# Two MLPs after linear attention in fp32 by three products: the first layer's blocks 7 and 8 as a pair by seven products of halves

## The chip, the core and the metric

The kernel runs on one core of a Trainium2 chip. The metric is the device time of one execution in microseconds, as the median of three runs. The engines are TensorE (PE in the rows, its weight loads PEld), VectorE (DVE), ScalarE (ACT), GpSimd (POOL) and SyncE (SP), which here only starts DMA transfers.

## What is computed

```python
kv = einsum('bhsd,bhse->bhde', k, v)           # 8 batches, 8 heads, 576 tokens, 64 wide
o  = einsum('bhsd,bhde->bhse', q, kv)
x  = o / sqrt(mean(o*o, -1) + 1e-6) * g_norm   # -> 4608 tokens x 512
h  = x @ w_in                                  # 512 x 2048
x1 = where(h >= 1, h, where(h <= -1, 0, (h + 1)**2 / 4)) @ w_out      # 2048 x 512
y  = maximum(x1 @ w_in2, 0)**2 @ w_out2
```

The weights come as 64-bit floats, which the kernel narrows to fp32 itself.

## The kernel before, in words

**Arithmetic.** A matrix of fp32 numbers is kept as a high part, rounded to TensorE's fp32r, and the rest, its low part. A product is three matmuls, high by high, high by low and low by high (`mm3`, L193 to 196; `mm_group`, L762 to 770 in the second layer). Making the two parts takes a cast on ScalarE and a subtraction on VectorE (`split`, `halve`).

**Blocks.** The 4608 tokens are nine blocks of 512: block b below 8 has the first 512 tokens of batch b, block 8 the last 64 tokens of every batch, which are gathered in DRAM (`xrd`). The first layer goes through the blocks in order, and each has 16 steps of 128 hidden features. A step issues `h_stage` (L576 to 597: 12 matmuls into one of two banks, then relu with a bias and a square on ScalarE, and a minimum and maximum on VectorE, giving u), `g_stage` (the two parts of u, named gs) and, two steps behind, `out_stage` (L606: 12 matmuls of gs and the step's output weights into four banks). Attention of batch b + 1 is made in block b, at fixed half-steps: `kv_stage`, `t_stage` (the transposed q), `o_stage` and `r_stage` (the norm). The results of a block go to DRAM (`x1d<-ev`), as does each batch's leftover (`xrd<-xrem`). In block 0 the first layer's weights are still being loaded, narrowed and split (`load_w`, `split_w`), beside attention 0 and 1.

**Second layer.** Blocks 0 to 7 go in four pairs. Pair n makes both of its blocks at once by seven products of halves (Strassen's scheme in Winograd's form, `PRODUCTS`, L73): tokens, inputs and hidden features are cut in two, sums of quarters are made of the inputs and of the weights, and 7 products stand where 8 would. `in_phase` (L783) makes the hidden features in four quarters of seven products by two feature steps; `out_phase` (L836) makes the seven output products one after the other. Each phase has 336 matmuls of 128x512. Block 8 follows as a plain block with streamed weights (`ws<-wcd`).

**Weights of the pairs.** The sums of the second layer's weights do not depend on the tokens. They are made in blocks 1 to 7 of the first layer by 16 jobs (`prep_load`, `prep_narrow`, `prep_sums`, `prep_split`, L264 to 316), one for each pair of weight tiles: load and narrow two tiles, four sums of 128x256, four splits, and stores to DRAM (`wsd<-s` for the products, `wcd<-s` whole for block 8), all started on SP's queue. The pairs then stream them, 512 KB at a time, through a ring of eight tiles (`ws<-wsd`). So that the jobs have room, the last six tiles of the first layer's output weights are stored as well (`wtd<-w`) and loaded again in each block (`wt<-wtd`).

**What sets the order.** The code is written in the order of a table of half-steps (`hook`), and a scheduler keeps this order on each engine but for priorities in the first block. All engines wait on semaphores and take their instructions in order. Tiles are handed round in pools and rings, so that a load waits until its tile is free. The transfers use eight semaphores in turn, over all queues, and a transfer is started only when the one that used its semaphore before has landed.

## Time and profile before

| | |
|---|---|
| median of three runs | 1597.66 us (1597.16 to 1598.02) |
| profiled execution, its own time | 1595.62 us |
| its span | 1593.8 us |
| TensorE busy, share of the span | 1577.4 us, 99% |
| VectorE, ScalarE, GpSimd busy | 949.1, 910.5, 111.0 us |
| mean DMA rate | 190 GB/s |

The span runs from the first to the last recorded instruction. Matmuls are pipelined and overlap in the records, so the pace of TensorE is read from the starts of groups of matmuls and not from the duration of one. In a timeline row the bracket at the end is idle time of the engine ahead of the row and what ended it.

### The profile page before, as it was taken

Reading aid. Unit: us, or ns where it says so; the run is one execution under the profiler, and the core shown is the slowest. Engines: PE = TensorE matmul, PEld = TensorE weight load, DVE = VectorE, ACT = ScalarE, POOL = GpSimd, SP = SyncE. Lnnn points to the kernel's source line nnn. Section 1 sums busy time; section 2 is a strip of 40 time slices with the busy share of each in tenths; the row PEclk is TensorE's granted clock in tenths of the full one; section 3 lists DMA queues with packets and bytes.
Section 4 is the critical chain, followed back from the end, with each engine's and each line's share of the span. In section 5 each row is a group of like instructions: output and inputs, shape, how many; then the busy total and the mean of one; then the engine's idle time right before and its main releaser. Section 6 shows DMA issues by size and latency. Waiting matters only on the chain.

```text
span 1593.8 us, 21182 instructions
## 1 busy us (share of the span) xinstructions
PE 1577.4 (99%) x7539; PEld 1292.1 (81%) x7541; DVE 949.1 (60%) x1574; ACT 910.5 (57%) x1661; POOL 111.0 (7%) x105
## 2 busy tenths in 40 slices
PE   9999999999999999999999999999999999999998
PEld 5678888888888888888888888888888888888886
DVE  6996656657666576643244348744974496457522
ACT  5986756667666676644344556456636663665321
POOL 0000000000000000000000121012101300330000
PEclk9999999999999999999999999999999999999999
DMA  9926567675776757522140557686768666865773
GB/s 285 280 83 174 195 170 228 179 239 174 228 215 186 235 177 230 182 73 90 53 145 29 170 194 242 194 219 222 237 195 243 218 216 198 243 219 186 201 239 102
DMA packets 306969, 302.36 MB, mean 190 GB/s; under 512 B 195504, under 2 KB 248752, under 8 KB 306864
## 3 DMA queue, kind: packets, MB, share of 16 engines
q1 hardware_dynamic: 304880, 300.22, 61.2%
q8 instruction: 60, 0.98, 0.2%
q10 hardware_dynamic: 1984, 0.79, 0.2%
q14 instruction: 45, 0.37, 0.1%
HBM read 231.74 MB, written 69.21 MB: 189 GB/s over the span
## 4 chain that ended last, share of the span: by engine, by line
PE 71%; issue 15%; DVE 9%; ACT 3%; POOL 1%; DMA 1%; DVEq 0%; SPq 0%; POOLq 0%; ACTq 0%
PE acc L196 26%; PE ph L196 26%; PE ph L770 10%; PE po L770 4%; DVE t L715 3%; DVE x L715 1%; PE po L196 1%; PE pkv L417 1%; POOL t L831 1%; DVE g L860 1%; PE pr L520 1%; DMA xr<-x1d 1%; DVE xr L738 1%; PE pwarm L1013 1%; ACT raw L226 1%
## 5 line engine op out<-in xcount | busy, mean ns | idle before, releaser
L196 PE MATMUL ph<-x,w 128*128 128x512 f32 x1728 | 418.9, 391 | 4.5 <-ACT w L175 2.0
L196 PEld LDWEIGHTS ph<-x,w 128*128 128x128 f32 x1728 | 321.7, 188 | 72.5 <-ACT w L175 2.9
L770 PE MATMUL po<-t,ws 128*128 128x512 f32 x1344 | 307.3, 391 | 1.7 <-DVE t L715 1.7
L770 PE MATMUL ph<-x,ws 128*128 128x512 f32 x1344 | 306.5, 390 | 0.7 <-DVE e L815 0.7
L770 PEld LDWEIGHTS po<-t,ws 128*128 128x128 f32 x1344 | 251.6, 188 | 56.7 <-DVE t L715 4.9
L770 PEld LDWEIGHTS ph<-x,ws 128*128 128x128 f32 x1344 | 252.2, 188 | 54.0 <-DVE e L815 1.9
L196 PE MATMUL acc<-gs,w 128*128 128x512 f32 x1152 | 281.2, 392 | 0.2 <-DVE u L594 0.2
L196 PEld LDWEIGHTS acc<-gs,w 128*128 128x128 f32 x1152 | 213.6, 188 | 43.7 <-DVE u L594 0.8
L592 ACT ACTIVATE u<-ph,halfb 128x512 f32<-128x512 f32 x144 | 99.3, 690 | 183.6 <-PE ph L196 183.2
L594 DVE SCALAR_TENSOR_TENSOR u<-u,ph 128x512 f32<-128x512 f32 x144 | 98.6, 684 | 167.7 <-ACT u L182 167.4
L715 DVE TENSOR_TENSOR t<-g,t 128x512 fp32r<-128x512 f32 x192 | 134.8, 708 | 74.2 <-ACT t L175 70.4
L175 ACT CAST t<-g 128x512 fp32r<-128x512 f32 x192 | 116.4, 620 | 71.8 <-DVE t L715 51.6
L188 DVE TENSOR_TENSOR gs<-u,gs 128x512 fp32r<-128x512 f32 x160 | 110.5, 690 | 62.2 <-ACT gs L175 61.3
L175 ACT CAST gs<-u 128x512 fp32r<-128x512 f32 x160 | 99.4, 621 | 74.4 <-DVE u L594 57.3
L196 PE MATMUL acc<-gs,wt 128*128 128x512 f32 x576 | 139.4, 391 | 0.0
L196 PEld LDWEIGHTS acc<-gs,wt 128*128 128x128 f32 x576 | 106.9, 188 | 21.5
L823 DVE TENSOR_TENSOR h<-ph,e 128x512 f32<-128x512 f32 x96 | 66.0, 691 | 55.9 <-PE ph L770 50.2
L824 ACT ACTIVATE h<-h 128x512 f32<-128x512 f32 x96 | 60.5, 630 | 60.0 <-DVE h L823 56.1
L182 ACT ACTIVATE u<-u 128x512 f32<-128x512 f32 x144 | 91.0, 632 | 2.0
L831 POOL TENSOR_TENSOR t<-g 128x512 f32<-128x512 f32 x32 | 43.1, 1346 | 633.7 <-ACT g L825 353.0
L825 ACT ACTIVATE g<-h 128x512 f32<-128x512 f32 x128 | 80.9, 632 | 3.6
L815 DVE TENSOR_TENSOR e<-ph,e 128x512 f32<-128x512 f32 x64 | 43.4, 688 | 44.3 <-PE ph L770 43.3
(108 smaller groups left out, 1427.3 us busy)
## 6 DMA issues: line engine op xcount, KB each, us to landing
ws<-wsd SPq DMA_DIRECT2D x224, 512.0 KB, 3.3
wsd<-s SPq DMA_DIRECT2D x112, 256.0 KB, 4.1
wt<-wtd SPq DMA_DIRECT2D x48, 512.0 KB, 4.5
raw<-in_moe_w_in_dram SPq DMA_DIRECT2D x32, 512.0 KB, 5.7
raw<-in_moe_w_out_dram SPq DMA_DIRECT2D x32, 512.0 KB, 5.5
wcd<-s SPq DMA_DIRECT2D x32, 512.0 KB, 3.2
ws<-wcd SPq DMA_DIRECT2D x32, 512.0 KB, 3.5
x1d<-ev SPq DMA_DIRECT2D x36, 256.0 KB, 3.1
```

The costliest lines, as they stand in the source:

```text
L175: return e.copy(dst, src)
L182: e.activation(dst, src, AF.Square)
L188: lo = engine(op + "_lo", phase).tensor_tensor(t[:, 1, :], src, t[:, 0, :].bitcast(F32), ALU.subtract)
L196: nc.tensor.matmul(dst, wt(a), xt(c), start=first and n == 0, stop=last and n == 2)
L592: nc.scalar.activation(u, ps, AF.Relu, bias=halfb, scale=0.5)
L594: nc.vector.scalar_tensor_tensor(u, u, 1.0, ps, op0=ALU.min, op1=ALU.max)
L715: engine2(op + "_lo").tensor_tensor(t[:, 1, :], src, t[:, 0, :].bitcast(F32), ALU.subtract)
L770: nc.tensor.matmul(ps, wt(a), xt(c), start=first and n == 0 and i == 0, stop=last and n == len(lhs) - 1 and i == 2, skip_group_check=True,)
L823: nc.vector.tensor_tensor(h, bank, add, ALU.add)
L824: nc.scalar.activation(h, h, AF.Relu)
L825: nc.scalar.activation(g, h, AF.Square)
L831: engine2("t_sum").tensor_tensor(t1[k], b, a, ALU.subtract)
```

## The change

The first layer's blocks 0 to 6 stay plain. Its blocks 7 and 8 are made as a pair, by the code that made the second layer's pairs, and the pairs run in this order: second layer 0 and 1, 2 and 3, first layer 7 and 8, second layer 4 and 5, 6 and 7. The second layer's block 8 is still plain.

- Attention 7, in block 6, writes its result to DRAM (`xpd`, from `xt`) and the pair loads its inputs from `xpd` and `xrd` as the others do from `x1d`.
- All streamed weights lie in one set of DRAM arrays, `wsd[layer, in or out, quarter]`, and tiles have the halves of features outside: `[128, half, high or low, 256]`. `wcd` and `wtd` are gone.
- The first layer's split weights are kept in DRAM as well (`keep_halves`, `keep_first`), and its sums are made by the same 16 jobs: `prep_join` adds the two parts of a tile again, `prep_sums` and two `prep_split` follow. All jobs are spread over 164 half-steps, from half-step 36, where they were spread over 104 steps.
- The tail of output weights that are loaded again in each block is nine tiles and not six; the jobs use five tiles of a ring and not three.
- The stores of sums, of kept weights and of the results of plain blocks are queued in a list (`owed`) and started half a step later on ScalarE's queue (`pay`).
- In the first layer's pair each of the four products of a feature step that end in the activation has relu with a bias and the square on ScalarE, and a minimum and maximum on VectorE. `put_out` stores its results without the transposes.

```diff
-    TAIL = 6
-    RING = 3
+    TAIL = 9
+    RING = 4
...
+    PLAIN = B - 1
+    PAIRS = [(2, 0), (2, 2), (1, PLAIN), (2, 4), (2, 6)]
...
+    def keep_halves(L, which, i, n, t):
+
+        made = MADE[which][2 * n : 2 * n + 2]
+        hs = slice(0, 2)
+        if L == 1 and None in made and not (which == 1 and i + n * NH >= NF - TAIL):
+            hs = slice(1, 2) if made[0] is None else slice(0, 1)
+        owed.append(
+            (wsd[L, which, i // 2][:, 2 * n + hs.start : 2 * n + hs.stop, i % 2], t[:, hs])
+        )
+
+    owed = []
+
+    def pay(n):
+
+        for dst, src in owed[:n]:
+            nc.scalar.dma_start(dst, src)
+        del owed[:n]
...
-            nc.sync.dma_start(wtd[f - (NF - TAIL)], t.rearrange("p a f -> p (a f)").bitcast(F32))
+            keep_halves(L, which, f % NH, f // NH, t.bitcast(F32))
...
+    def prep_join(L, which, i):
+
+        for n in range(2):
+            f = i + n * NH
+            t = prep.get((L, which, i, n))
+            if t is not None:
+                d, w = t[:, :, 0, :], t
+            else:
+                w = (wi[L, f] if which == 0 else wo[L, f]).bitcast(F32)
+                d = d_tile(f"j_{which}_{f}").rearrange("p (h f) -> p h f", h=2)
+            nc.vector.tensor_tensor(d, w[:, :, 0, :], w[:, :, 1, :], ALU.add)
+            prep[L, which, i, n] = d
...
+    def prep_split(L, which, i, n):
+        src = prep.pop((L, which, i, n))
+        t = prep_tile(f"s{L}_{which}_{i}_{n}", [P, 2, 2, H2], F32R)
+        split_halves(t, src, engine2("s_hi"), engine2("s_lo"))
+        keep_halves(L, which, i, n, t.bitcast(F32))
+
+    def keep_first(which, f):
+
+        t = wi[1, f] if which == 0 else wo[1, f]
+        keep_halves(1, which, f % NH, f // NH, t.bitcast(F32))
...
-        norm(t, y, o)
-        nc.gpsimd.tensor_copy(xrem[b][:, hp, :], t[:, TB:])
-        split(xs[1, b][hp], t[:, :TB], "x", b)
+        if b < LAST_B:
+            norm(t, y, o)
+            nc.gpsimd.tensor_copy(xrem[b][:, hp, :], t[:, TB:])
+            split(xs[1, b][hp], t[:, :TB], "x", b)
+            return
...
         if L == 1:
-            nc.sync.dma_start(x1d[b][:, c, :], t)
+            owed.append((x1d[b][:, c, :], t))
...
+                        if PAIRS[n][0] == 1:
+                            nc.scalar.activation(g, h, AF.Relu, bias=halfb, scale=0.5)
+                            nc.scalar.activation(g, g, AF.Square)
+                            nc.vector.scalar_tensor_tensor(g, g, 1.0, h, op0=ALU.min, op1=ALU.max)
...
+    jobs = [(0, store_xrem, 0)]
+    for b in range(1, B):
+        jobs += attention(b, 2 * NF * (b - 1), 7, range(NP))
+    for job in sorted(jobs, key=lambda j: j[0]):
+        hook(*job)
...
+    kept = [(w, f) for f in range(NF) for w in range(2) if w == 0 or f < NF - TAIL]
+    for j, (w, f) in enumerate(kept):
+        hook(2 * (NF + 2) + 3 * j, keep_first, w, f)
...
-        s0 = NF + 2 + (7 * j * (7 * NF - 8)) // (7 * 2 * NH)
...
+        s0 = 2 * NF + 4 + (j * 164) // 16
```

Three places of the order in which the engines get their instructions stand here, the kernel before first and the changed kernel second. A row has the line, the operation and output<-inputs; in the names the first number is the block of u, gs and ph or which weight of raw, d and w (0 in, 1 out), the next the step or tile, and the last only tells copies apart.

VectorE in block 0, from u of step 7 to u of step 8, before (the names t_1, kvbd and wk are attention 1):

```order
L594 SCALAR_TENSOR_TENSOR u_0_7_1095<-u_0_7_1095,ph_0_7_1082 128x512
L188 TENSOR_TENSOR gs_0_6_1058<-u_0_6_1027,gs_0_6_1058 128x512
L454 SCALAR_TENSOR_TENSOR t_1_1040<-pr_1_0_1031,t_1_1040 128x288
L454 SCALAR_TENSOR_TENSOR t_1_1040<-pr_1_1_1035,t_1_1040 128x288
L188 TENSOR_TENSOR gs_0_7_1142<-u_0_7_1095,gs_0_7_1142 128x512
L457 SCALAR_TENSOR_TENSOR t_1_1040<-t_1_1040,wk_1_1_849 128x576
L594 SCALAR_TENSOR_TENSOR u_0_8_1180<-u_0_8_1180,ph_0_8_1167 128x512
```

The same engine and place now, the last twelve of the 26 rows from u of step 7 to u of step 8:

```order
L174 TENSOR_TENSOR w_0_11_864<-d_0_11_861,w_0_11_864 128x2x256
L219 TENSOR_TENSOR x_1_1_689<-t_1_964,x_1_1_689 128x512
L259 TENSOR_SCALAR d_0_12_976<-raw_0_12_858 128x512
L477 TENSOR_TENSOR kvbd_129<-pkv_2_1024,kvbd_129 64x64
L260 SCALAR_TENSOR_TENSOR d_0_12_976<-raw_0_12_858,d_0_12_976 128x512
L538 STREAM_TRANSPOSE qf_2_1041<-q_2_775 128x576
L259 TENSOR_SCALAR d_0_13_1061<-raw_0_13_973 128x512
L174 TENSOR_TENSOR w_0_12_979<-d_0_12_976,w_0_12_979 128x2x256
L540 TENSOR_TENSOR qT_1_2_1043<-qf_2_1041,qT_1_2_1042 128x576
L260 SCALAR_TENSOR_TENSOR d_0_13_1061<-raw_0_13_973,d_0_13_1061 128x512
L259 TENSOR_SCALAR d_1_10_1086<-raw_1_10_823 128x512
L676 SCALAR_TENSOR_TENSOR u_0_8_1105<-u_0_8_1105,ph_0_8_1092 128x512
```

Narrowing and splitting of the weight tiles 11 to 13, the norm of attention 1 and the start of its next head pair now stand ahead of u of step 8.

ScalarE in steps 4 and 5 of block 0, before (qT, s and wk are attention 1):

```order
L175 CAST w_1_3_683<-d_1_3_680 128x512
L182 ACTIVATE u_0_3_810<-u_0_3_810 128x512
L592 ACTIVATE u_0_4_879<-ph_0_4_866,halfb 128x512
L182 ACTIVATE u_0_4_879<-u_0_4_879 128x512
L175 CAST qT_1_0_660<-qf_0_659 128x576
L175 CAST gs_0_2_767<-u_0_2_754 128x512
L503 ACTIVATE s_1_0_703<-po_0_0_704 128x288
```

And now:

```order
L206 CAST w_1_3_601<-d_1_3_598 128x2x256
L213 ACTIVATE u_0_3_733<-u_0_3_733 128x512
L674 ACTIVATE u_0_4_802<-ph_0_4_789,halfb 128x512
L167 DMA wsd_1_0_108<-w_1_0_485 128x512
L206 CAST qT_1_0_567<-qf_0_566 128x576
L213 ACTIVATE u_0_4_802<-u_0_4_802 128x512
L206 CAST w_1_4_656<-d_1_4_653 128x2x256
L206 CAST gs_0_2_685<-u_0_2_672 128x512
L167 DMA wsd_1_0_108<-w_1_1_499 128x512
L553 ACTIVATE s_1_0_621<-po_0_0_622 128x288
```

Two stores of kept weight tiles stand between ScalarE's instructions; such rows come back through blocks 0 to 6, 156 more transfers on this queue in all.

SP in block 0, before, from the second head pair's loads of attention 1 on:

```order
L357 DMA k_1_625<-in_k_dram 128x8x64
L364 DMA rest_205<-in_k_dram 64x2x64
L360 DMA v_1_628<-in_v_dram 128x2x256
L364 DMA rest_205<-in_v_dram 64x2x64
L373 DMA q_1_631<-in_q_dram 32x18x32 x4
L567 DMA xrd<-xrem_296 512x1x64
L208 DMA raw_0_7_665<-in_moe_w_in_dram 128x4x256
```

And now, from the last weight load that is ahead of them:

```order
L244 DMA raw_1_5_518<-in_moe_w_out_dram 128x1024
L649 DMA xrd<-xrem_219 512x1x64
L407 DMA k_0_538<-in_k_dram 128x8x64
L414 DMA rest_127<-in_k_dram 64x2x64
L410 DMA v_0_541<-in_v_dram 128x2x256
L414 DMA rest_127<-in_v_dram 64x2x64
L423 DMA q_0_559<-in_q_dram 32x18x32 x4
```

The store of block 0's leftover moved from behind the loads of both head pairs to ahead of the first.

## Rows read from the trace of the kernel before

**Rows 1.** The page's busy times by engine, and its chain by engine.

```profile
PE 1577.4 (99%) x7539; PEld 1292.1 (81%) x7541; DVE 949.1 (60%) x1574; ACT 910.5 (57%) x1661; POOL 111.0 (7%) x105
...
PE 71%; issue 15%; DVE 9%; ACT 3%; POOL 1%; DMA 1%; DVEq 0%; SPq 0%; POOLq 0%; ACTq 0%
```

**Rows 2.** Timeline of TensorE, plain block, first pair: start, us, instructions, count.

```profile
725.42 2.88 PE L196 MATMUL acc<-gs,w 128*128 128x512 f32 x12
728.14 2.88 PE L196 MATMUL ph<-x,w 128*128 128x512 f32 x12
...
891.34 70.88 PE L770 MATMUL ph<-x,ws 128*128 128x512 f32 x312
```

**Rows 3.** The same timeline from one pair's second phase to the next one's.

```profile
962.05 26.50 PE L770 MATMUL po<-t,ws 128*128 128x512 f32 x115
988.79 50.39 PE L770 MATMUL po<-t,ws 128*128 128x512 f32 x221 [0.23 <-DVE t L715]
...
1085.64 30.26 PE L770 MATMUL ph<-x,ws 128*128 128x512 f32 x132 [0.22 <-DVE e L815]
1115.73 26.48 PE L770 MATMUL po<-t,ws 128*128 128x512 f32 x115
```

**Rows 4.** Stretches: length, busy us of five engines, clock, DMA share, GB/s.

```profile
40.00:60.00 20.00, 17.16 (x89) 12.27 (x88) 19.56 (x38) 18.95 (x40) 0.00 (x0) 1.00 0.96 265
80.00:100.00 20.00, 19.43 (x103) 15.18 (x102) 19.15 (x36) 17.74 (x37) 0.76 (x1) 1.00 0.08 26
322.00:418.00 96.00, 96.00 (x507) 80.04 (x506) 63.15 (x113) 64.75 (x127) 1.35 (x4) 1.00 0.70 218
891.00:962.00 71.00, 71.00 (x315) 58.85 (x314) 32.50 (x48) 44.52 (x73) 17.89 (x12) 1.00 0.61 203
962.00:1037.00 75.00, 74.77 (x329) 61.21 (x329) 63.40 (x97) 41.41 (x73) 6.31 (x4) 1.00 0.66 217
```

**Rows 5.** Timeline of TensorE in the first block.

```profile
45.56 0.69 PE L417 MATMUL pkv<-v,k 128*64 128x64 f32 x16
...
51.54 3.35 PE L196 MATMUL ph<-x,w 128*128 128x512 f32 x12 [1.54 <-ACT w L175]
...
93.51 1.52 PE L196 MATMUL ph<-x,w 128*128 128x512 f32 x6
...
101.02 3.06 PE L196 MATMUL ph<-x,w 128*128 128x512 f32 x12 [0.96 <-DVE u L594]
```

**Rows 6.** Costliest groups: count, busy us, mean ns of one, idle before and releaser.

```profile
L592 ACT ACTIVATE u<-ph,halfb 128x512 f32<-128x512 f32 x144 | 99.3, 690 | 183.6 <-PE ph L196 183.2
L594 DVE SCALAR_TENSOR_TENSOR u<-u,ph 128x512 f32<-128x512 f32 x144 | 98.6, 684 | 167.7 <-ACT u L182 167.4
L831 POOL TENSOR_TENSOR t<-g 128x512 f32<-128x512 f32 x32 | 43.1, 1346 | 633.7 <-ACT g L825 353.0
L229 DVE SCALAR_TENSOR_TENSOR d<-raw,d 128x512 int32<-128x512 int32 x64 | 43.5, 686 | 5.3 <-ACT raw L226 4.2
L228 DVE TENSOR_SCALAR d<-raw 128x512 int32<-128x512 int32 x64 | 26.4, 417 | 10.6 <-DMA raw<-in_moe_w_in_dram 7.0 <-DMA raw<-in_moe_w_out_dram 3.6
L296 DVE TENSOR_TENSOR s<-s,d 128x256 f32<-128x256 f32 x16 | 6.7, 418 | 0.0
```

**Rows 7.** Timelines of GpSimd, SP's queue and, last, ScalarE with its queue.

```profile
38.35 0.24 POOL L479 COPY xrem<-t 128x64 f32<-128x64 f32 x1 [2.76 <-DVE t L458]
...
27.30 0.61 SPq L357 DMA_DIRECT2D k<-in_k_dram  x1
...
43.30 0.58 SPq L567 DMA_DIRECT2D xrd<-xrem  x1
...
340.72 0.47 SPq L314 DMA_DIRECT2D wsd<-s  x1
...
341.74 7.68 SPq L314 DMA_DIRECT2D wsd<-s  x6
...
1587.70 0.58 ACT L626 COPY ev<-acc 128x512 f32<-128x512 f32 x1 [0.77 <-PE acc L196]
1587.76 2.00 ACTq L636 DMA_DIRECT2D out_dram<-ev  x3
```

More of the change, by code (lines that the diff above doesn't have):

```diff
@@ L325, in linear_attention_rms_two_mlps @@
     og = {}
+    turn = {}
     banks = itertools.cycle(
@@ L535, in new_x, with begin, attention_first @@
         ]
-    def attention(b):
+    def begin(b):
+        if b < LAST_B:
+            new_x(1, b)
+        xrem[b] = ap2.tile([P, KD, REM], F32, tag="xrem", name=f"xrem_{b}")
+    def attention_first():
         slots = {}
@@ L676, in tile @@
             return pool.tile(shape, dtype, tag=tag, name=name)
-    w_ring = Ring(*((wp, f"w1_{(NF - RING + i) % NF}") for i in range(8)))
+    w_ring = Ring(*((wp, f"w1_{i}") for i in (0, 1, 2, 3, 4, 13, 14, 15)))
     t_ring = Ring(*[(gp, "g")] * 3, (wp, f"w0_{NF - 2}"), (wp, f"w0_{NF - 1}"))
@@ L912, in put_out @@
     def put_out(n, hn, hm):
+        L, b0 = PAIRS[n]
+        b = b0 + hn
+        if L == 1:
+            for m in range(2):
+                nc.sync.dma_start(x1d[b][:, 2 * hm + m, :], result[n](hm, m, hn))
+            return
         t = t_ring.tile([P, 2, TB], F32, f"ov{n}_{hn}_{hm}")
-        b = 2 * n + hn
         for m in range(2):
@@ new lines, in hook @@
+    def hook(s, f, *a):
+        hooks.setdefault((s // 2, s % 2), []).append((f, a))
+    jobs = [(0, store_xrem, 0)]
[3 more added lines that the diff above has]
+        hook(*job)
+    for i in range(NF):
+        later = split_later if i < 2 else split_w
+        for w, ahead, at in ((0, 7, 6), (1, 6, 3)):
+            if i + ahead < NF:
+                hook(2 * i + w, load_w, 1, i + ahead, w)
+            if i + at < NF:
+                hook(2 * i + w, later, 1, i + at, w)
@@ L994, in linear_attention_rms_two_mlps @@
-    last = (NB - 1) * NF
+        s0 = 2 * NF + 4 + (j * 164) // 16
+        for d, L, f, a in (
+            (-3, 2, prep_load, ()),
+            (2, 2, prep_narrow, (0,)),
+            (3, 2, prep_narrow, (1,)),
+            (4, 2, prep_sums, ()),
+            (4, 2, prep_split, (0,)),
+            (5, 2, prep_split, (1,)),
+            (5, 1, prep_load, ()),
+            (6, 2, prep_split, (2,)),
+            (7, 2, prep_split, (3,)),
+            (8, 1, prep_join, ()),
+            (9, 1, prep_sums, ()),
+            (9, 1, prep_split, (2,)),
+            (10, 1, prep_split, (3,)),
+        ):
+            hook(s0 + d, f, L, which, i, *a)
@@ L995, in linear_attention_rms_two_mlps @@
+    last = 2 * (PLAIN - 1) * NF
     first_x = x2_jobs(0, Ring(*[(st, "st")] * 7))
@@ L997, in linear_attention_rms_two_mlps @@
     for t, f in zip(when, first_x):
-        hook(0, last + t, 1, f)
-    for i in range(7):
-        hook(0, last - 3 + i if i < 3 else last + i, 1, load_w2)
+        hook(last + 2 * t + 1, f)
+    for i, t in enumerate((7, 9, 11, 13, 15, 21, 23)):
+        hook(last + t, load_w2)
     nc.scalar.preload_act_table_set("natural_log_exp_and_others")
@@ L1029, in linear_attention_rms_two_mlps @@
     nc.vector.memset(halfb, 0.5)
-    first = attention(0)
+    first = attention_first()
     for s, n in WARMS:
```

268 lines of the change are left out of this document (127 added, 141 removed).

## The prediction

> **What bounds the kernel now.** I read the totals of the page first, then the chain that ended last [rows 1]: TensorE is busy for 99% of the span, and the chain is mostly TensorE too, so a change is worth what it takes off TensorE or puts in front of it. The TensorE timeline of a plain block comes next [rows 2]: groups of twelve matmuls follow each other every 2.72 us without an idle mark, 0.2267 us per matmul, and in the pairs 312 of them fill 70.9 us at the same pace. The same timeline over a whole pair [rows 3] shows what a pair costs: out-phases start at 962.05 and 1115.73, so 153.68 us for its 672 matmuls, against 672 x 0.2267 = 152.3; the 1.4 us between are a few short waits, such as 0.23 for t and 0.22 for e. The table of stretches [rows 4] shows how full VectorE and ScalarE are beside it: in the fourth plain block (322 to 418) 63.2 and 64.8 of 96 us with DMA at 0.70, in a pair's second phase 63.4 and 41.4 of 75, but from 40 to 60 19.6 and 19.0 of 20. Only there, in the first block, does TensorE wait now: 1.54 us for a weight at 51.54, 0.96 for u at 101.02 [rows 5]. The granted clock is 1.00 in every stretch, the level of 2.4 GHz.
>
> **The products removed and added.** Blocks 7 and 8 of the first layer cost 2 x 384 = 768 matmuls as plain blocks and 672 as a pair. Removed: 768 x 0.2267 = 174.1 us, all in stretches where TensorE never idled [rows 2]. Added: a fifth pair at 153.7 [rows 3]. Attention 7 stays in the block before, and its TensorE work is the same. The sum is -20.4 us.
> The trace prices a matmul at 226.7 ns at the granted clock of 1.00 [rows 2]. The Trainium skill (TensorE: Matmul & The Clock Gate, section "Wait — 56ns, not 53.3ns?") gives 215.7 ns for 512 columns; by it the 96 matmuls would be worth 20.7 us and not 21.8. The trace decides, and it is 5% above the page.
>
> **VectorE and ScalarE in blocks 1 to 5.** Each of sixteen jobs now also sums a first-layer weight pair: two joins and two splits of 512 columns and four sums of 256, so 4 x 0.69 + 4 x 0.418 = 4.4 us of VectorE [rows 6]. The jobs lie closer, 3.12 to a block where there were 2.46, and a second-layer job is 2 x (0.417 + 0.686) + 4 x 0.418 + 4 x 0.69 = 6.6 us. So a block gains 3.12 x 4.4 + 0.66 x 6.6 = 18 us of VectorE: 63 becomes 81 of 96. ScalarE gains some ten casts or scalings at up to 0.69, 7 us, and, because the stores move from SP's queue to its own, 22 to 26 transfer starts. No row shows a start on ScalarE in a busy stretch. The nearest are the end of the run, where three starts last 2.00 us, 0.67 each, beside a copy that runs at 1587.70 for 0.58, and SP's starts of the same stores, 0.47 alone, or 7.68 for six, 1.28 each, when they queue [rows 7]. If the starts run beside the arithmetic, as the two rows at 1587.7 suggest, ScalarE stands at 72; if each holds it for 0.47 to 0.67, at 83 to 89. Neither engine is full on average. What counts is how late it may be. A step's u must be done before the product two steps on takes the same bank, three groups of 2.72 = 8.2 us after the step's product ends, and it needs three instructions of 0.69, 2.1; the output product reads gs 10.9 us after, and that needs two more, 3.5 us. So 6 to 7 us of backlog are free. In the order, the densest two steps hold 15.8 us of VectorE work against 12.2 of TensorE, a backlog of 3.6: covered in the main chain, but beyond the 2.5 to 3 us that the attention's norms have. Bounds 0 and 8 us over five blocks; I take 1.3, near the lower end, since no full block loses anything now.
>
> **The first block.** Here there is no cover [rows 4, 5]. The order puts 24 VectorE instructions between u of steps 7 and 8, where five stood. Following their widths at 0.42 to 0.69 apiece, u of step 8 ends near 94.9, and the product that needs its bank started at 93.51: 1.4 us. Some 14 stores of kept weight tiles now start on ScalarE ahead of block 1: 14 x 0.47 = 6.6 us if all are exposed, nothing if none. On SP the store of block 0's leftover tokens now stands ahead of block 1's k, v and q loads. Its data is ready after the last copy, 38.35 + 0.24, and SP waits in order; before, k started at 27.30 and the store at 43.30, behind them [rows 7]. The loads so start up to 11 us later, and the first product on them ran at 45.56 [rows 5]: with some 2.5 us of starts and a landing of 4 to 5 us it is just met, or late by 1 to 3. The weight loads behind have 15 us to spare. Bounds 0 and 9; I take 2, half of what stands exposed above, since these delays overlap where TensorE waits already.
>
> **The first layer as a pair.** Its activation needs one more VectorE instruction for each of 32 products, 32 x 0.69 = 22 us in the first phase [rows 6]. There VectorE was busy for 32.5 of 71 us [rows 4] and goes to 55. GpSimd's differences, 1.35 us apiece [rows 6], come later by a VectorE delay, and the second phase waits for their results at its first products. A quarter of that phase holds 18 VectorE instructions, 12.4 us; the first also has the eight transposes of the pair before, 5.5 us, so 17.9 of its 84 x 0.2267 = 19.0 us are taken. Bounds 0 and 4, I take 1: a pair already waits some 0.2 at such a place [rows 3]. Its output needs no transposes, which frees 5.5 us beside work that hides it.
>
> **Sum.** 1595.62 - 20.4 + 1.3 + 2 + 1 = 1579.5 in the profiled execution, which lies 2.0 below the median of the runs; so 1581.6 on the median.
>
> **Rivals.** (1) Full gain: every addition is hidden, 1597.66 - 20.4 = 1577.3. For it: no idle mark in any full block. Against it: the first block, where both engines are above 90%.
> (2) First block and backlog at their upper ends: 1577.3 + 9 + 3 to 5 = 1590. For it: 19.6 of 20 us of VectorE [rows 4] and an order that piles up exactly there; against: most of what is added has no reader before the pairs.
> (3) Slower: ScalarE becomes the bound because each start holds its arithmetic, and holds it longer when it has to wait. By the program each start waits for the transfer that began eight starts before it, on either queue, so a store on ScalarE can stand behind a load of SP; behind it are queued the casts and u of the next step, for which VectorE and then TensorE wait. About 118 starts lie in blocks 1 to 5. At SP's queued price of 1.28 [rows 7] that is 151 us of ScalarE, 30 a block: 72 + 30 = 102 of 96, with 6 us a block on TensorE at the least, and with the bursts uncovered about 8: 1577.3 + 5 x 8 = 1617. It turns slower from 0.20 us per start that reaches TensorE, (1600.9 - 1577.3) / 118. Against it: a mean ScalarE load of 72 to 89, 6 us of backlog that are free, and that nothing waits in a stretch with 0.70 of DMA.
> The two rows at 1587.7 show an instruction of ScalarE running while its queue starts transfers. The Trainium skill (DMA: Bandwidth & Descriptors, section "Anatomy of one DMA — SWDGE (gpsimd) path") says that DMA engines do not wait on semaphores and that such a wait happens on the issuing sequencer before dispatch. By that rule the waits above stand on ScalarE's sequencer, which is rival 3's mechanism; no row here shows a start that waits on ScalarE, and I keep it small because the waited-for transfers are several microseconds old.
> (4) The change does not do what it says. The order has 2688 + 3360 such matmuls where there were 3456 + 2688, 96 fewer; that leaves this nothing.
>
> **How the numbers follow.** Forecast, with 2 to 8 us of cost, 1579 to 1585: 0.50. Rival 1, 1576 to 1579: 0.20. Rival 2, 1585 to 1594: 0.18. All costs at their bounds, 1577.3 + 21 = 1598, within 0.2% (3.2 us, about what a measurement of this kernel can tell from no change): 0.06. Rival 3: 0.06. Faster is 0.88. A range of 1576 to 1592 holds the first two and most of the third, some 0.83.
>
> **What would show it.** Right: out-phase to out-phase 153 to 155 us for the first layer's pair; blocks 1 to 5 still 96 us each without idle marks on TensorE; the first block longer by about 2 us, with the waits near 45, 55 and 94. Wrong: groups of twelve at more than 2.72 us in blocks 1 to 5 with ScalarE named as releaser (rival 3), or a first block longer by 7 or more (rival 2), or a fifth pair above 158.

## The result and the profile after

| | before | after |
|---|---|---|
| median | 1597.41 us (1596.64 to 1598.02) | 1607.17 us (1604.97 to 1607.73) |
| profiled execution, its span | 1595.62, 1593.8 us | 1607.73, 1605.9 us |
| mean granted clock | 0.999 | 0.991 |

The ratio is 1.0063, with an interval of 1.0051 to 1.0075: slower by 0.6%, where 1.0% faster was forecast. The page of after, its busy times by engine, beside [rows 1]:

```profile
PE 1567.6 (98%) x7443; PEld 1279.8 (80%) x7445; DVE 1071.9 (67%) x1806; ACT 943.4 (59%) x1731; POOL 134.7 (8%) x117
```

The 96 matmuls are gone (7539 to 7443). TensorE's busy time fell by 9.8 us only, though, and the span grew by 12.1, so 32.5 us of idle time and slow matmuls have come in. Three marks in time place them. The first copy of block 0's results, in the timelines of VectorE of before and of after:

```profile
141.95 0.69 DVE L624 COPY ev<-acc 128x512 f32<-128x512 f32 x1 [3.18 <-PE acc L196]
```

```profile
153.87 0.69 DVE L707 COPY ev<-acc 128x512 f32<-128x512 f32 x1 [0.39 <-PE acc L227]
```

And TensorE's timeline of after in the pairs, which answers to [rows 2, 3]:

```profile
816.35 26.48 PE L853 MATMUL po<-t,ws 128*128 128x512 f32 x115
...
969.99 26.57 PE L853 MATMUL po<-t,ws 128*128 128x512 f32 x115
996.78 50.39 PE L853 MATMUL po<-t,ws 128*128 128x512 f32 x221 [0.21 <-DVE t L789]
...
1095.33 30.24 PE L853 MATMUL ph<-x,ws 128*128 128x512 f32 x132 [1.92 <-DVE e L898]
1125.40 26.17 PE L853 MATMUL po<-t,ws 128*128 128x512 f32 x109
...
1154.19 50.39 PE L853 MATMUL po<-t,ws 128*128 128x512 f32 x221 [0.72 <-DVE t L789]
```

- **Block 0**: 141.95 to 153.87, so 11.9 us lost.
- **Blocks 1 to 6**: the first pair's out-phase started at 962.05 [rows 3]. Less two plain blocks of 384 matmuls at 0.2267, 174.1, it should start at 787.9; it starts at 816.35. That is 28.4 lost by then, 16.5 behind block 0. Blocks 1 to 5 alone, between the first copies of the results of blocks 0 and 5, took 621.46 - 141.95 = 479.5 before and take 646.34 - 153.87 = 492.5, so 13.0 of the 16.5 lie there.
- **The pairs and block 8**: from there to the end 1593.8 - 962.05 + 153.7 = 785.45 was due, and it is 789.55, so 4.1 lost. The first layer's pair takes 1154.19 - 996.78 = 157.4 between the second rows of the two out-phases, and 1125.40 - 969.99 = 155.4 between their first rows, where [rows 3] has 153.7; the other 2.0 are lost inside its out-phase.

11.9 + 16.5 + 4.1 = 32.5, less 20.4, is the 12.1 us.

**Block 0.** The table of stretches of after (length, busy us and instructions of PE, PEld, DVE, ACT, POOL, clock, DMA share, GB/s), beside [rows 4]; the last row lies in blocks 3 and 4:

```profile
40.00:60.00 20.00, 17.70 (x86) 13.12 (x85) 19.39 (x38) 18.50 (x38) 0.00 (x0) 0.91 0.74 190
80.00:100.00 20.00, 17.86 (x82) 13.50 (x82) 15.62 (x30) 12.40 (x24) 0.24 (x1) 0.83 0.90 304
436.00:534.00 98.00, 90.78 (x472) 75.48 (x469) 65.90 (x124) 60.90 (x123) 1.83 (x4) 0.97 0.70 217
```

From 80 to 100 VectorE and ScalarE are less busy than before (15.62 and 12.40 us against 19.15 and 17.74), while DMA's share is 0.90 against 0.08. Work that was done early before is now being waited for. What SP's queue waits for between 40 and 145 us (total, times, longest):

```profile
SPq L239 <- DMA wsd<-w: 13.4, 2, 7.1
SPq L244 <- DMA wsd<-w: 12.4, 3, 8.4
SPq L423 <- DMA wsd<-w: 9.6, 3, 4.7
...
SPq L414 <- DMA wsd<-w: 4.5, 2, 4.3
SPq L410 <- DMA wsd<-w: 3.6, 3, 1.8
```

SP's loads of weights (L239, L244), k, v and q wait 43.5 us in all for stores of kept weights, which start on another queue, ScalarE's. In before SP waited in block 0 too, 40.4 us for VectorE's w, but the longest of these waits, 23.2, ended at 97.8, when its weight loads were far ahead: behind the first thirteen, 14 had started from 43.9 to 61.4. In after these 14 start from 56.1 to 90.2. TensorE's timeline of after, beside [rows 5]:

```profile
51.92 4.92 PE L227 MATMUL ph<-x,w 128*128 128x512 f32 x12 [1.61 <-ACT w L206]
...
82.91 3.78 PE L227 MATMUL acc<-gs,w 128*128 128x512 f32 x8 [0.96 <-DVE gs L219]
...
117.60 3.68 PE L227 MATMUL ph<-x,w 128*128 128x512 f32 x8 [3.40 <-DVE u L676]
...
471.32 0.61 PE L227 MATMUL po<-qT,kvbd 128*128 128x288 f32 x1 [7.21 <-ACT qT L206]
```

The waits themselves are short. Behind them TensorE runs slowly: 12 matmuls last 4.92 us, 8 last 3.78 and 3.68, and the granted clock of the two stretches is 0.91 and 0.83, between the levels of 1.2 and 2.4 GHz, where it was 1.00. At full pace a row of twelve lasts 2.88 [rows 2], and one of eight four starts of 0.2267 less, 1.97. So 2.0 + 1.8 + 1.7 = 5.6 us are lost to the clock in the first, second and third of these places, nearly as much as the 1.61 + 0.96 + 3.40 = 6.0 of the waits.

**Blocks 1 to 6.** TensorE stops for more than half a microsecond four times here, for 0.58, 1.49, 7.21 and 2.87 us; before, it never did. These are 12.2 of the 16.5 us. The longest wait is 7.21 us at 471.32, in the last of the three stretches above; there too the clock is below 1.00, at 0.97. The timeline around it, SP's queue, VectorE and ScalarE:

```profile
450.82 0.37 SPq L311 DMA_DIRECT2D raw<-in_moe_w_in_dram  x1
...
455.51 0.43 DVE L259 TENSOR_SCALAR d<-raw 128x512 int32<-128x512 int32 x1 [6.08 <-DMA raw<-in_moe_w_in_dram]
...
463.27 0.37 SPq L311 DMA_DIRECT2D raw<-in_moe_w_in_dram  x1
...
468.67 0.43 DVE L259 TENSOR_SCALAR d<-raw 128x512 int32<-128x512 int32 x1 [5.00 <-DMA raw<-in_moe_w_in_dram]
...
470.60 0.67 ACT L206 CAST qT<-qf 128x576 fp32r<-128x576 f32 x1 [5.26 <-DVE qf L538]
```

and SP's waits from 436 to 476:

```profile
SPq L311 <- DMA wsd<-s: 10.3, 2, 8.7
```

A job's raw load takes a tile of the ring (`prep_tile`) that held sums, and so waits up to 8.7 us on SP for the store of these sums to land. The second raw load of the same job starts 12.4 us after the first, with a load of wt and seven of k and v in between. VectorE reaches the narrowing (L259) before the data does, stops for 6.08 and 5.00 us, and all that is queued behind it, here the transpose qf that gives qT, comes late. Such waits of VectorE for weights on the way, over the blocks of after:

```profile
DVE d L259 <- DMA raw<-in_moe_w_in_dram: 22.1, 10, 6.1
...
DVE d L259 <- DMA raw<-in_moe_w_out_dram: 4.7, 1, 4.7
...
DVE wf L329 <- DMA wf<-wsd: 3.5, 1, 3.5
```

Together 30.3 us; before had two rows of the kind, 7.0 and 3.6 [rows 6]. Few of these waits reach TensorE: the two above, and one of 4.69 at 356.54 ahead of the stop of 1.49 us.

The stop of 2.87 us in block 6 has another cause. ScalarE's copy of a result of block 5 waits until the store of another result has landed, and such stores are now started by ScalarE itself, later than before. TensorE's timeline and ScalarE's:

```profile
655.43 0.96 PE L227 MATMUL acc<-gs,w 128*128 128x512 f32 x3 [2.87 <-ACT ev L709]
```

```profile
650.47 0.33 ACTq L167 DMA_DIRECT2D x1d<-ev  x1
654.79 0.59 ACT L709 COPY ev<-acc 128x512 f32<-128x512 f32 x1 [3.69 <-DMA x1d<-ev]
```

**The pair.** VectorE's timeline of after ahead of the wait at 1095.33:

```profile
1093.98 0.69 DVE L945 TENSOR_TENSOR g<-g,t 128x512 f32<-128x512 f32 x1 [1.39 <-POOL t L919]
1094.59 1.28 DVE L898 TENSOR_TENSOR e<-ph,e 128x512 f32<-128x512 f32 x2
```

GpSimd's difference t is late, VectorE waits 1.39 us for it, and e, which TensorE needs, is queued behind.

### The profile page after: what moved, and what is told of

It is laid out like the page before. It is cut to its first block, busy times and chain, and to the rows that moved or that the text cites. A ratio compares the mean times of both kernels' runs of the same rounds, so it can differ in the third digit from the quotient of the medians.

```text
span 1605.9 us, 21544 instructions
## 1 busy us (share of the span) xinstructions
PE 1567.6 (98%) x7443; PEld 1279.8 (80%) x7445; DVE 1071.9 (67%) x1806; ACT 943.4 (59%) x1731; POOL 134.7 (8%) x117
## 5 line engine op out<-in xcount | busy, mean ns | idle before, releaser
L853 PE MATMUL po<-t,ws 128*128 128x512 f32 x1680 | 385.7, 390 | 4.1 <-DVE t L789 3.9
L853 PE MATMUL ph<-x,ws 128*128 128x512 f32 x1680 | 382.8, 389 | 2.3 <-DVE e L898 2.3
L853 PEld LDWEIGHTS po<-t,ws 128*128 128x128 f32 x1680 | 314.1, 188 | 74.9 <-DVE t L789 9.6
L853 PEld LDWEIGHTS ph<-x,ws 128*128 128x128 f32 x1680 | 315.1, 188 | 68.9 <-DVE e L898 3.6
L227 PE MATMUL ph<-x,w 128*128 128x512 f32 x1344 | 335.1, 397 | 6.7 <-DVE u L676 4.3
L227 PEld LDWEIGHTS ph<-x,w 128*128 128x128 f32 x1344 | 254.0, 191 | 61.3 <-DVE u L676 4.6
L789 DVE TENSOR_TENSOR t<-g,t 128x512 fp32r<-128x512 f32 x240 | 169.3, 711 | 80.6 <-ACT t L206 78.6
L206 ACT CAST t<-g 128x512 fp32r<-128x512 f32 x240 | 145.3, 621 | 89.6 <-DVE t L789 61.4
L227 PE MATMUL acc<-gs,w 128*128 128x512 f32 x696 | 174.0, 395 | 3.8 <-ACT ev L709 2.9
L227 PEld LDWEIGHTS acc<-gs,w 128*128 128x128 f32 x696 | 128.9, 189 | 30.4 <-ACT ev L709 3.2
L206 ACT CAST x<-xr 128x512 fp32r<-128x512 f32 x74 | 45.9, 622 | 49.8 <-DVE xr L821 35.3
```

Source lines behind the costliest of these rows:

```text
L206: return e.copy(dst, src)
L227: nc.tensor.matmul(dst, wt(a), xt(c), start=first and n == 0, stop=last and n == 2)
L789: engine2(op + "_lo").tensor_tensor(t[:, 1, :], src, t[:, 0, :].bitcast(F32), ALU.subtract)
L853: nc.tensor.matmul(ps, wt(a), xt(c), start=first and n == 0 and i == 0, stop=last and n == len(lhs) - 1 and i == 2, skip_group_check=True,)
```

## The experiments

The theories, by the letters of the expectations. **A**: the starts on ScalarE cost the time, because they hold its arithmetic (the forecast's rival 3) and because they share semaphores with SP's loads. **B**: the added arithmetic of VectorE and ScalarE costs it. **C**: the loads of second-layer weights come late, from e7 on because they wait for a ring tile whose store has to land. **D** and **E** are for block 0: the stores of kept tiles hold up SP's loads, by DMA time and semaphores (D) or by the shared semaphores alone (E).

In the table, block 0 is its loss by the copy's mark against 141.95, blocks 1 to 6 the loss behind it by the out-phase's mark against 787.9; then VectorE's waits for loads of job weights (raw and wf, over the whole run), and SP's waits for `wsd<-w` from 40 to 145. All in us. Marks and waits are those of one execution of each kernel. The executions of e11_ring4 alone lie between 1592.48 and 1601.36, so a difference of a few us between two marks shows nothing by itself.

| run | median | ratio and interval | block 0 | blocks 1 to 6 | VectorE for loads | SP for stores |
|---|---|---|---|---|---|---|
| after | 1607.17 | 1.0063 (1.0051 to 1.0075) | 11.9 | 16.5 | 30.3 | 43.5 |
| e1_pool | 1630.20 | 1.0208 (1.0192 to 1.0223) | 4.1 | 47.1 | 39.6 | 0 |
| e2_sp | 1644.12 | 1.0297 (1.0282 to 1.0313) | 4.2 | 60.7 | 1.1 | 0 |
| e3_no_first | 1594.33 | 0.9987 (0.9978 to 0.9997) | 9.9 | 7.8 | 39.6 | 45.8 |
| e4_no_store | 1595.73 | 0.9995 (0.9985 to 1.0005) | 6.6 | 8.1 | 21.2 | 42.6 |
| e5_late_keep | 1607.01 | 1.0071 (1.0055 to 1.0087) | 9.0 | 20.1 | 43.3 | 45.2 |
| e6_loads_first | 1606.98 | 1.0067 (1.0045 to 1.0089) | 11.9 | 15.0 | 29.3 | 47.5 |
| e7_ring6 | 1588.67 | 0.9953 (0.9937 to 0.9969) | 7.8 | 1.1 | 19.6 | 42.6 |
| e8_three | 1607.17 | 1.0068 (1.0052 to 1.0084) | 6.5 | 21.1 | 36.3 | 46.0 |
| e9_keep_pool | 1589.79 | 0.9963 (0.9951 to 0.9975) | 3.3 | 6.2 | 29.7 | 0 |
| e10_ring7 | 1606.87 | 1.0053 (1.0033 to 1.0074) | 14.9 | 12.4 | 29.7 | 39.5 |
| e11_ring4 | 1597.60 | 1.0007 (0.9995 to 1.0019) | 10.5 | 10.2 | 64.3 | 40.1 |
| e12_pair_dve | 1584.02 | 0.9919 (0.9905 to 0.9934) | 3.7 | 6.2 | 29.3 | 0 |
| e13_own_raw | 1601.08 | 1.0029 (1.0017 to 1.0041) | 13.8 | 6.6 | 15.6 | 41.0 |
| e14_own_raw_pool | 1579.16 | 0.9894 (0.9877 to 0.9910) | 4.0 | 1.6 | 13.3 | 0 |
| e15_narrow_later | 1597.17 | 1.0002 (0.9993 to 1.0012) | 11.4 | 4.0 | 17.2 | 44.3 |
| e16_shift | 1606.76 | 1.0068 (1.0053 to 1.0083) | 14.0 | 12.6 | 35.2 | 45.9 |

### The owed stores started on another queue

```diff
-            nc.scalar.dma_start(dst, src)
+            nc.gpsimd.dma_start(dst, src)   # e1_pool
+            nc.sync.dma_start(dst, src)     # e2_sp
```

> The changed kernel with the stores of kept tiles, sums and plain results started on GpSimd's queue instead of ScalarE's; the same transfers, no work left out. In the program GpSimd's transfers use eight semaphores of their own, so a store no longer waits for a load of SP eight starts before, nor a load for a store. Theory A (the starts on ScalarE, their waits and their coupling with SP's loads cost the time): block 0 ends near 145 to 148 us instead of 153.9, blocks 1 to 6 lose 5 us or less instead of 16, 1582 to 1590 us in all. Theory B (the added VectorE and ScalarE work is what makes TensorE wait): 1603 to 1608, and the waits on transfers in ScalarE's rows go while TensorE's stay.

> The changed kernel with the same stores started on SP's queue, at the same places of the program; no work left out. SP's queue was the place of the stores before the change. Theory A: ScalarE loses nothing to starts, but loads stand behind stores on SP; block 0 near 144, since the kept tiles are stored later there, and the blocks lose less than 16, 1583 to 1595 in all. Theory B: 1603 to 1608. Theory C (loads of second-layer weights come too late because SP's queue is blocked by what stands ahead of them): slower than the changed kernel, 1610 or more.

Both are far slower than before, by 2.1 and 3.0%. No theory had e1 there, and e2 is where C put it. Of the three queues, ScalarE's is the best for all of these stores. In the trace of after a start on ScalarE can run beside its arithmetic, as in the last two rows, a cast and a start at 461 us. But a start that has to wait holds ScalarE up, as in the first two:

```profile
455.51 0.33 ACTq L167 DMA_DIRECT2D x1d<-ev  x1
455.88 0.50 ACT L571 ACTIVATE wk<-pr,lnb 128x288 f32<-128x288 f32 x1 [4.00 <-DMA raw<-in_moe_w_in_dram]
...
461.64 0.62 ACT L206 CAST gs<-u 128x512 fp32r<-128x512 f32 x1 [0.96 <-DVE u L676]
461.65 0.37 ACTq L167 DMA_DIRECT2D wsd<-s  x1
```

ScalarE idles for 4.00 us until a load that SP started has landed, starts a store at 455.51 and goes on. This is the picture of A and of rival 3. In blocks 1 to 6 of after there are five such waits for which no other reason shows, 9.2 us in all; none of them is the last link to a stop of TensorE. So A is real but small there, and e7 and e15 below leave all starts on ScalarE and lose 1.1 and 4.0 in the blocks.

In both e1 and e2, block 0 loses 4 us and not 12, and SP's waits for stores there are gone. That speaks for the coupling of stores and loads in block 0 (A's second half, later E). The price comes later, since in-order queues now hold other work behind a store. With the stores on SP they wait there for the data, and every load behind waits with them (SP's waits of e2_sp from 145 to 740):

```profile
SPq L167 <- DVE s L174: 131.2, 22, 18.8
SPq L167 <- DVE d L259: 64.8, 8, 18.8
```

### The first layer's halves left out

```diff
-            nc.sync.dma_start(t.bitcast(F32), wsd[L, which, a][:, MADE[which].index(p)])
+            nc.sync.dma_start(t.bitcast(F32), wsd[2, which, a][:, MADE[which].index(p)])
-    for j, (w, f) in enumerate(kept):
+    for j, (w, f) in enumerate(kept[:0]):
+            if L == 2:                      # e3_no_first: no first-layer jobs
                 hook(s0 + d, f, L, which, i, *a)
+        if L == 2:                          # e4_no_store: jobs made, not stored
+            keep_halves(L, which, i, n, t.bitcast(F32))
```

> The changed kernel without the preparation of the first layer's weights: its sums are not made, its tiles are not kept but for the nine of the tail, and the first layer's pair streams the second layer's stored weights instead, so its values are not the reference's. The pairs, the denser second-layer jobs and the stores on ScalarE stay. Theories A and B both: block 0 near 144 and blocks 1 to 6 with 2 us of loss or less, 1579 to 1584. If the denser second-layer jobs or the shorter lead of their loads cost the time (theory C), 1590 or more.

> The changed kernel with the first layer's sums made on VectorE and ScalarE in the same half-steps, but neither the sums nor the kept tiles (other than the nine of the tail) stored; the first layer's pair streams the second layer's stored weights instead, so its values are not the reference's. It leaves out 72 transfer starts and keeps the arithmetic. Theory A: near the kernel without any of it, 1580 to 1588. Theory B: near the changed kernel in blocks 1 to 6, 1595 to 1600 (block 0 gets its kept stores off in either theory).

Without any of the first layer's halves 12.8 us come back, and with their arithmetic but without their stores 11.4. The two intervals overlap, so the 4.4 us of VectorE per job that the forecast priced cost nothing that shows, and B falls, although 1595.73 lies in the range that it gave for e4. But 17.7 and 14.7 us of loss are left in block 0 and blocks 1 to 6 with the halves gone. In e3_no_first only nine starts of kept tiles, those of the tail, remain on ScalarE in block 0, and SP waits 45.8 us for them; in the blocks VectorE waits 39.6 us for loads.

### The prediction's order on SP, and later starts

```diff
+        with tc.issue_after(last_gs[-1].ins) if last_gs else ExitStack():   # e5_late_keep
+            for dst, src in owed[:n]:
+                nc.scalar.dma_start(dst, src)
-    for job in sorted(jobs, key=lambda j: j[0]):                            # e6_loads_first
+    for job in sorted(jobs, key=lambda j: (j[0], j[0] == 0 and j[1] not in (load_kv, load_q))):
```

> The changed kernel with one thing undone: the stores of kept first-layer tiles and all other stores of the list may not be moved ahead of the cast of the step in which they are written, so none of the 15 tiles beside the tail's is stored in block 0. All the work is there. Theory D (in block 0 the kept stores take DMA time and semaphores from SP's loads of weights, which then come late): block 0 ends near 147 to 149 us instead of 153.9 and the whole is 5 us shorter, 1600 to 1603. If the added time of block 0 is the order on VectorE alone: 1606 to 1608.

> The changed kernel with one thing undone: on SP the store of block 0's leftover stands behind the loads of both head pairs of block 1 again, as before the change. Nothing else is moved by hand. By the step of the prediction that costed it at up to 3 us: 1604 to 1606, with the k, v and q loads about 11 us earlier. If it also sets the order of VectorE and ScalarE in the first steps, and with it the wait of 2.9 us for gs near 82 us: 1602.

The leftover's store ahead of block 1's loads, for which the forecast had 1 to 3 us, costs nothing: with the loads ahead (k starts at 33.24 and not at 39.36) block 0 ends at 153.84 against 153.87. Starting the stores behind the cast of gs saves 2.9 us in block 0, less than D gave it, and loses 3.6 in the blocks. SP still waits 45.2 us in block 0 for the nine stores of the tail; the other stores of kept tiles now start later, in blocks 1 and 2, where the jobs' loads are, and VectorE's waits go from 30.3 to 43.3.

### The length of the ring

```diff
-    TAIL = 9     # five ring tiles
+    TAIL = 10    # e7_ring6; 11 in e10_ring7, 8 in e11_ring4
```

> The changed kernel with a tail of ten tiles instead of nine, so that the jobs of blocks 1 to 6 go round six tiles and not five; each block loads one tile more again, 512 KB. Theory C (a load of second-layer weights waits on SP for a ring tile whose store has not landed, comes late, and VectorE's narrowing waits for it with u, gs and the attention behind it): VectorE's waits for these loads fall from 26.8 us to under 10, blocks 1 to 6 lose 6 us or less instead of 16, 1596 to 1600. Theory B (too much VectorE and ScalarE work): 1606 to 1610.

> All three together: kept stores not moved into block 0, the leftover's store behind the loads, and six ring tiles. If theories C and D hold and the parts add: 1607 - 5 - 2 - 9 = 1591, 1587 to 1595; faster than before the change. If the parts hide one another: 1598 to 1603.

> The changed kernel with a tail of eleven tiles, so seven ring tiles instead of five. Theory C: no more to be had than with six in blocks 1 to 6, where nothing waited any more; 1586 to 1590, the difference from six lying in block 0. If the gain of six was something else of the longer tail (fewer kept stores, another order in block 0): again 5 us or more less, 1583 or below.

> The changed kernel with a tail of eight tiles, so four ring tiles instead of five: the suspected wait made longer. Theory C: VectorE waits over 60 us for the loads of second-layer weights instead of 27, blocks 1 to 6 lose 35 us or more instead of 16, 1625 to 1660. If the ring is not the cause: 1603 to 1610.

Six tiles instead of five take some 18 us off, most of it in the blocks (16.5 to 1.1). I took this for the cause, the wait for a free tile. The next runs spoke against it, and missed what C gave for them: seven tiles are as slow as five, four are faster than five, and six together with the edits of e5 and e6 give 1607.17 again. VectorE's waits in e7 also fell only to 19.6 us; but TensorE, which stops for 12.2 us in these blocks of after, stops for 0.7 there. More tiles are not simply better. I take it that ring length shifts when each load becomes possible and which work is queued ahead of it; no run shows that by itself. With four tiles VectorE waits 64.3 us for loads and yet 10.2 are lost, so such a wait costs only where it reaches TensorE.

### Raw loads with tiles of their own, and later narrowing

```diff
-    TAIL = 9
+    TAIL = 11
+    raw_tags = itertools.cycle(range(NF - TAIL + RING, NF - TAIL + RING + 2))      # e13_own_raw
-            t = prep_tile(f"raw2_{which}_{f}", [P, 2 * TB], I32)
+            t = wp.tile([P, 2 * TB], I32, tag=f"w1_{next(raw_tags)}", name=f"raw2_{which}_{f}")
-            (2, 2, prep_narrow, (0,)),        # and all steps behind it
+            (4, 2, prep_narrow, (0,)),        # e15_narrow_later: two half-steps later
-        s0 = 2 * NF + 4 + (j * 164) // 16
+        s0 = 2 * NF + 5 + (j * 164) // 16     # e16_shift: loads and all, one half-step later
```

> The changed kernel with a tail of eleven tiles, as in the run with seven ring tiles, but two of the seven kept for the loads of second-layer weights alone, so that such a load never waits for a store; the stores go round the other five. If late loads are the cause: VectorE waits for them under 5 us in all (8.0 with seven, 26.8 with five), blocks 1 to 5 lose under 3 us beside 479.5 before the change (13.0 with five, 7.2 with seven); block 0 as with seven, 155 to 157, so 1597 to 1601. If the places of any wait are what counts: 1604 to 1610.

> The changed kernel with five ring tiles, its jobs' loads where they were and every step after them two half-steps, 5.4 us, later, so that a load has longer before VectorE's narrowing asks for it. If late loads are the cause: VectorE's wait for them falls from 26.8 to under 12 us and the whole to 1597 to 1602, block 0 unchanged at 154. But the stores come later as well, and the loads that wait for them with them: if that is the loop, 1605 to 1610.

> The changed kernel with all jobs one half-step later and nothing else changed: a control. If the cost of blocks 1 to 6 is set by how long loads wait: 1606 to 1609. If it is set by where a wait happens to meet TensorE: anywhere from 1597 to 1615, clear of 1607 by 3 us or more.

These three were to separate a late load from a mere shift. e13_own_raw has the seven tiles of e10_ring7, but two of them serve raw loads alone, so that a raw load never waits for a store of sums; VectorE's waits for raw go to 2.4 us, and the blocks lose 6.6 instead of 12.4. The gain isn't the raw loads', though. The two long stops of TensorE in e10 are 3.81 us behind a wait for wf and 3.93 behind a copy of a result that waits for a store. In e13 the first is still there, 3.47, since its wf loads are still in the shared ring, where VectorE waits 13.2 us for them; the second is down to 1.23, and why isn't known.

e15_narrow_later is the clean one. It keeps five tiles and every raw load where it was, and what follows the raw loads comes two half-steps later: VectorE waits 17.2 us instead of 30.3, the blocks lose 4.0 instead of 16.5, and the whole is 10 us faster than after. The stop of 7.21 us is gone. e16_shift moves loads and work together by one half-step: the waits stay (35.2), and so does the time, 1606.76. In part this is luck, since block 0 loses 2.1 more and the blocks 3.9 less. But the longest stop of TensorE is left in its trace at the same place:

```profile
471.84 0.61 PE L227 MATMUL po<-qT,kvbd 128*128 128x288 f32 x1 [5.92 <-ACT qT L206]
```

So for the longest stop the distance from load to use decides, as C says, and not the place of the jobs. The stop for the copy of a result is another matter; it is 2.27 us in e15 and 0.91 in e16.

### Block 0, the pair, and all together

```diff
+            + ((nc.gpsimd,) if L == 1 and n < 2 else ())      # e9_keep_pool, with TAIL = 10:
+        for dst, src, *e in owed[:n]:                         # kept first-layer tiles on GpSimd
+            (e[0] if e else nc.scalar).dma_start(dst, src)
-                engine2("t_sum").tensor_tensor(t1[k], b, a, ALU.subtract)
-                engine2("t_sum").tensor_tensor(b, d, b, ALU.subtract)
+                e2 = nc.vector if PAIRS[n][0] == 1 else nc.gpsimd     # e12_pair_dve: e9 and this
+                e2.tensor_tensor(t1[k], b, a, ALU.subtract)
+                e2.tensor_tensor(b, d, b, ALU.subtract)
                                                               # e14_own_raw_pool: e12 and e13
```

> The kernel with six ring tiles, and the stores of kept first-layer tiles started on GpSimd's queue, whose transfers have eight semaphores of their own; the stores of sums and results stay on ScalarE. The block 0 of the changed kernel and of the one with six ring tiles has SP's loads waiting some 40 us for those stores, eight starts before them, and the weight loads start 12 to 30 us late. Theory E (this coupling is what block 0 pays): SP waits for no store of kept tiles, block 0 ends at 145 to 147 instead of 149.8, and the whole is 1584 to 1587 against 1588.7. If block 0 pays for the DMA time of the stores or for the order on VectorE: 1588 to 1592.

> The same with the two differences of each of eight feature steps of the first layer's pair made on VectorE instead of GpSimd, 16 instructions of 0.69 us for 16 of 1.3 and 1.8. If the 1.9 us that TensorE waits in this pair (for e, behind a VectorE instruction that waits for GpSimd) and the 0.75 in its second phase come from GpSimd's lateness: 2 us less than the kernel before it in this list, 1582 to 1585, the pair 155 instead of 157.4. If VectorE is then the bound there: the same or 1 to 3 us more.

> The same tiles of their own in the kernel that stores the kept tiles from GpSimd's queue and makes the first pair's differences on VectorE, which took 1584.0 with a ring of six. If late loads are what its blocks 1 to 5 still lose (6.6 us): 1578 to 1581, all of the matmuls' gain but block 0's 3 us. If not: 1583 to 1587.

e9_keep_pool differs from e7_ring6 in the queue of the kept tiles alone: SP's waits for them go from 42.6 to 0, and block 0 loses 3.3 instead of 7.8. The stores are the same in both, and from 40 to 145 ScalarE waits for a transfer once in e7, for 0.9 us, so neither their DMA time nor A's first half explains the gain, and E holds in block 0. The blocks lose 6.2 instead of 1.1, so the time is the same, 1589.79, and not the 1584 to 1587 that E gave. e12_pair_dve takes 5.8 us off that: with t from VectorE the whole out-phase of the first layer's pair runs without a wait (336 matmuls in one row of TensorE's timeline), and so does its in-phase:

```profile
1104.66 76.32 PE L854 MATMUL po<-t,ws 128*128 128x512 f32 x336
```

e14_own_raw_pool has all three mends. It beats both kernels: 1579.16 us, 1.06% below before. Its page, then its TensorE timeline:

```profile
PE 1558.6 (99%) x7445; PEld 1274.9 (81%) x7445; DVE 1075.3 (68%) x1822; ACT 943.6 (60%) x1731; POOL 132.9 (8%) x133
```

```profile
81.42 3.78 PE L228 MATMUL acc<-gs,w 128*128 128x512 f32 x8 [2.90 <-DVE gs L220]
...
974.13 50.41 PE L855 MATMUL po<-t,ws 128*128 128x512 f32 x221 [0.33 <-DVE t L791]
1024.38 76.32 PE L855 MATMUL ph<-x,ws 128*128 128x512 f32 x336
1100.54 76.32 PE L855 MATMUL po<-t,ws 128*128 128x512 f32 x336
1176.69 76.32 PE L855 MATMUL ph<-x,ws 128*128 128x512 f32 x336
```

The first layer's pair takes 1176.69 - 1024.38 = 152.3 us, which is 672 x 0.2267: it waits for nothing, where [rows 3] has 153.7 for the second layer's. Against e12 the raw loads' own tiles, with a tail of eleven, take another 4.9 us off: VectorE's waits for raw go from 23.3 to 0, and TensorE's stops in blocks 1 to 6 from 4.9 to 0.5. Against the span of before: -20.4 for the matmuls, +4.0 in block 0, +1.6 in blocks 1 to 6, -1.4 in the pairs and block 8, together -16.2 (1577.5 against 1593.8). VectorE is as full as in after, 68 and 67%. The added arithmetic is all there, and it is hidden.

## Why the prediction was wrong

**The products.** Right: 96 matmuls fewer, 20.4 us by marks and pace; e14_own_raw_pool shows them in its span.

**Blocks 1 to 5, +1.3 with bounds of 0 and 8.** This is the step that failed most; it measured 13.0, and 16.5 with block 6. I priced the instructions of VectorE and ScalarE and the starts on ScalarE, and asked how late these engines might be. The loads were taken as there when needed. Of the row that showed otherwise, VectorE's narrowing waiting 7.0 and 3.6 us for raw [rows 6], I used the duration only. The jobs' loads lie on SP behind k and v, in tiles that must be stored first, and with more stores, on another queue, they came later than the narrowing, which stands in order ahead of u, gs and the attention. e15 with its control shows this for the longest stop, 7.21 us, and e14 beside e12 agrees, though its tail is longer by a tile; e3 and e4 show that the priced 4.4 us a job was not it. That VectorE would be busy 81 of 96 us was too high, too: in e14, where nothing of the work is left out, it is 71 to 74 in these blocks. A second stop, 2.87 us for a copy of a result behind a late store, wasn't in the forecast at all. No full block losing anything before was no bound: the 10.6 us of waits for raw were there before, but none reached TensorE.

**The first block, +2 with bounds of 0 and 9.** It measured 11.9. "The weight loads behind have 15 us to spare" is the sentence that failed. They had it against the starts I counted, but not against the stores on ScalarE: 43.5 us of waits on SP. I had written the rule down, in rival 3: each start waits for the transfer eight starts before, on either queue. But I applied it only to a store behind a load, never to a load behind a store. The Trainium skill (DMA: Bandwidth & Descriptors, section "Anatomy of one DMA — SWDGE (gpsimd) path") puts such a wait on the issuing sequencer, ahead of dispatch; the rows agree, with SP's sequencer as the one that waits. The forecast's 14 stores were too few as well: 26 of kept tiles start by 150.6 us. e9, against e7, takes these waits away and 4.5 us of block 0 with them. How much block 0 loses doesn't follow their sum, though: 39.5 to 47.5 us of them go with 6.5 to 14.9 lost. Of after's 11.9, 3.3 to 4.2 are left in every version without them, 2.90 for gs near 81 among it. I put that down to the new order of VectorE's work (the forecast's 1.4), but it was not tried apart. The store on SP was priced at 1 to 3 us and costs nothing (e6).

**The pair, +1 with bounds of 0 and 4.** The mechanism was right, GpSimd's differences come late and a VectorE instruction that TensorE needs stands behind them, and the size was off: 3.7 us and not 1, inside the bounds. Out-phase to out-phase, the mark I gave, it is 155.4 against 153 to 155. The waits of 1.92 and 0.72 us come ahead of the last 132 matmuls of the in-phase and behind 115 of the out-phase, where [rows 3] has 0.2 in other pairs. Taking t off GpSimd gives 5.8 us on the medians, more than the 3.7, because the small waits that other pairs have go too: 152.3 instead of 157.4.

**The rivals.** Rival 3 had the right sign and nearly the right price, 28.4 us over some 118 starts, 0.24 each against the 0.20 from which it decides. That is luck. Its mechanism can be seen, ScalarE held by a start that waits, but at five places and for 9.2 us in blocks 1 to 6, and no stop of TensorE ends with it; e7 loses 1.1 there with all these starts in place. Rival 2 had block 0 and a backlog at 13 us in sum, where 28.4 came. I gave both 0.24, since I looked for what could fill an engine. Behind block 0 no engine filled up, and the queue of loads wasn't among my engines.

**What stays open.** Why late loads reach TensorE with five and seven ring tiles, and less with four and six, isn't settled. The VectorE waits alone don't tell it: under 20 us of them 1.1 to 6.6 are lost (e2_sp apart, whose loss is on SP), from 21 to 43 us 6.2 to 21.1 but for e1_pool, and with 64.3 only 10.2. Nor is it settled why the blocks lose 5 us more in e9 than in e7, or what sets the stop for the copy of a result, 0.9 to 3.9 us in seven of the kernels with these stores on ScalarE.

## What to carry to other kernels

A change that adds stores also has to be priced on the queue that loads: list every load behind a tile that must be stored first or behind a transfer that shares its semaphore, and compare its landing with the instruction that reads it, on an engine that works in order. Keep tiles that are loaded apart from tiles that are stored (with one tile more, 4.9 us between e12 and e14), and leave the reader some distance behind the load: two half-steps gave back 10 us here. Sums of waits on an engine off the critical path say little; follow each stop of the engine that bounds the kernel back to its cause. One setting that mends a kernel (six tiles) is no proof of the cause, as its neighbours showed.

## What the hardware showed beside this

- The clock after the same pause wasn't the same in all profiles. At 51.92 in after TensorE waits 1.61 us, and the next twelve matmuls last 4.92; in e7_ring6 (TensorE's timeline) they last 3.35 behind the same wait at the same time:

```profile
51.91 3.35 PE L227 MATMUL ph<-x,w 128*128 128x512 f32 x12 [1.61 <-ACT w L206]
```

  The granted clock from 40 to 60 is 0.91 in after and 1.00 in e7. Of the 18 kernels, before [rows 5] and ten others are like e7 (3.32 to 3.37), and in after, e2, e3, e5, e13 and e15 the twelve last 4.5 to 4.9. Each was profiled in one execution, so whether the kernel decides it or the execution isn't known.
- Starts are not alike. One on ScalarE lasted 0.37 us beside a cast. On GpSimd one lasted 0.73 us in e1_pool, behind an idle time of 2.36 that the row puts down to VectorE's t, which this transfer doesn't store; the reason isn't known:

```profile
267.27 0.73 POOL L167 DMA_DIRECT2D wsd<-s  x1 [2.36 <-DVE t L507]
```
